# Value matmuls by seven block products, woven with the gate matmuls, and GpSimd taking over the spread sums

## The chip, the cores and the metric

The kernel runs on one core of a Trainium2 chip. The metric is the device time of one launch in microseconds (us). In one set of rounds nine executions of the kernel before lay within 0.3% of each other (546.1 to 547.48 us). One core has five engines that matter: TensorE (PE in the profile; PEld is its weight load), VectorE (DVE), ScalarE (ACT), GpSimd (POOL) and SyncE (SP), which here only issues DMAs.

## The reference

Eight batches of attention with projected keys and values are followed by a gated feed-forward layer over all 8192 tokens.

```python
k_proj = einsum('ks,bhsd->bhkd', E, k)           # 8 batches, 8 heads, 1024 -> 64 positions
v_proj = einsum('ks,bhsd->bhkd', F, v)
attn   = softmax(q @ k_proj.T / 8)
x      = (attn @ v_proj)                         # reshaped to 8192 tokens x 512
gate   = 1 / (1 + exp(-(x @ w_gate)))            # 512 -> 1536
val    = x @ w_val                               # 512 -> 1536
out    = (gate * val) @ w_out                    # 1536 -> 512
```

Nearly all of the arithmetic lies in the last three products. The kernel works on 16 blocks of 512 tokens, two for each batch.

## The kernel before

The output product already uses a Strassen-like scheme: a 2x2 block product by seven instead of eight smaller products, with sums of the operands made first ("spread sums" S1 to S4 of the hidden layer, T1 to T4 of the weights). The gate and the value still use plain matmuls.

```python
def mstep(blk, m):                     # one feature tile: 4 gate and 4 value matmuls, 512 columns
    pbs = {n: ffn.next() for n in "GV"}
    for n in "GV":
        for i in range(NI):
            mm_one(blk, m, i, n, pbs[n])
    gate(blk, m, pbs["G"], pbs["V"])   # tanh on ACT, (1 + t) * value on DVE

def s_sums(blk, n, ms):                # the sums of the hidden layer, on VectorE
    ...
    o, a, b, op, r, w = {
        1: (S1, A21, A22, ALU.add, "A21 A22", "S1"),
        2: (S2, S1, A11, ALU.subtract, "S1 A11", "S2"),
        3: (A21, A11, A21, ALU.subtract, "A11 A21", "A21"),
        4: (A12, A12, S2, ALU.subtract, "A12 S2", "A12"),
    }[n]
    dve(lambda e: e.tensor_tensor(o, a, b, op), ...)

def first_products(blk):               # the first five of the seven output products
    product(blk, a, "A11", "B11", True)
    keep_snap(0, a)
    product(blk, c, "A12", "B21", True, True)
    add_snap(0, c, 0, 0)
    for ms in ((0, 3), (3, 6)):
        s_sums(blk, 4, ms)
    product(blk, a, "S2", "T2")        # the third: reads S2
    keep_snap(1, a)
    product(blk, c, "S1", "T1", True)
    product(blk, a, "A21", "T3")       # the fifth: reads S3, which lies in A21
    ...

def gather():                          # reciprocals of the softmax sums to four partitions
    for i in range(4):
        add("SP", lambda e, i=i: e.dma_start(rrow[::32, i, :], rden[i::32, :]), ...)

def spread(rnd):                       # ... and from there to all: 16 broadcasts on GpSimd
    for j in range(4):
        n = 4 * rnd + j
        for c, parts in ((1, P), (0, 64)):
            pool(lambda e, ...: e.partition_broadcast(rb[0:parts, n, :], rrow[...], channels=parts), ...)

def mul(r, g, bk=None):                # attention outputs times the spread reciprocals
    dve(lambda e: e.tensor_tensor(xT[s][...], xu[:, n, :], rb[:, n, :], ALU.mult), ...)
```

Everything is placed by hand: `put(i, fn)` hangs a piece of attention behind the i-th feature tile. Each engine gets its instructions in program order, and semaphores are set wherever one engine needs what another made. A product of TensorE stands in a bank; an eviction is the instruction of ScalarE or VectorE that takes it out, so that the bank comes free for another product, and a snapshot is a copy taken in this way.

The softmax here doesn't subtract the row's maximum and nothing guards it: scores larger than these inputs give would overflow.

Of the kernel before, what the change touches and what calls it, by code (L numbers as in the profile page):

```python
# [118 lines left out]
def bass_linformer_attn__then__ffn_glu_sigmoid_kernel(  # L119
# [18 lines left out]
    with contextlib.ExitStack() as es:  # L138
# [5 lines left out]
        count = sbuf("count", [P, P], FP32)  # L144
        quad = sbuf("quad", [P, 1], FP32)
        row_f = sbuf("row_f", [P, 1], FP32)
        pats = sbuf("pats", [P, 4, 32], FP32)
        rows = sbuf("rows", [P, 4, 32], FP32)
        half = sbuf("half", [P, 2], FP32)
        identf = sbuf("identf", [P, P], FP32)  # L150
        ident = sbuf("ident", [P, P], BF16)
        dsel = sbuf("dsel", [P, 2, 2, 32], BF16)
        dsel8 = sbuf("dsel8", [P, 2, 4, 32], BF16)
        bsel8 = sbuf("bsel8", [P, 4, 2, 64], BF16)
        bsel8f = sbuf("bsel8f", [P, 4, 2, 64], FP32)
# [5 lines left out]
        KV = [sbuf(f"KV{i}", [P, H, S // P * DH], BF16) for i in range(2)]  # L161
        kp = sbuf("kp", [P, NR, DH], BF16)
# [5 lines left out]
        rden = sbuf("rden", [P, 512], FP32)  # L168
        rhi = sbuf("rhi", [P, 512], BF16)
        rhl = sbuf("rhl", [P, 512], BF16)  # L170
# [4 lines left out]
        rb = sbuf("rb", [P, 8, 512], FP32)  # L175
# [6 lines left out]
        sig = [sbuf(f"sig{i}", [P, 512], FP32) for i in range(3)]  # L182
# [4 lines left out]
        snap = [EF[:, 0:512], EF[:, 512:1024], sbuf("snap2", [P, 512], FP32)[:, :]]  # L187

# [28 lines left out]
        ffn, att = Ring(FB), Ring(AB)  # L217

# [119 lines left out]
        def constants():  # L338
# [61 lines left out]
            for t, k, m, w in ((dsel8, "dsel8", 8, 4), (dsel, "dsel", 4, 2)):  # L400
                for n in range(2):
                    for i in range(w):
                        dve(
                            lambda e, t=t, m=m, n=n, i=i: e.tensor_scalar(
                                t[:, n, i, :].rearrange("p (a b) -> p a b", b=m),
                                count[:, 0:m].unsqueeze(1).to_broadcast([P, 32 // m, m]),
                                half[:, n : n + 1],
                                2.0 * i,
                                op0=ALU.subtract,
                                op1=ALU.is_equal,  # L410
                            ),
                            ["count", ("half", n)],
                            [(k, n)],
                        )
# [117 lines left out]
        def half_unit(hf, ring):  # L532
# [86 lines left out]
            def bc(R):  # L619
# [17 lines left out]
                def keep(g):  # L637
                    act(
                        rb[:, 2 * R + g, :],
                        bank[bks[g]][:, :],  # L640
                        [],
                        [("rb", 2 * R + g)],
# [19 lines left out]
            def xo(R):  # L662
# [14 lines left out]
                for g in range(2):  # L677
# [3 lines left out]
                    elif R == 0:  # L681
                        scale(R, g, bank[bks[g]], rb[:, n, :], [("rb", n)], bks[g])
                if hf == 0 and R == 1:
                    for r in (2, 3):
                        for g in range(2):
# [5 lines left out]
                                    rb[:, 2 * R + g, cc],  # L691
                                    ALU.mult,
                                ),
                                [("rb", 2 * R + g)],
# [57 lines left out]
        def keep_vd(bk):  # L752
            for g in range(2):
                act(
                    vpD[64 * g : 64 * g + 64, :, :].rearrange("p h d -> p (h d)"),
                    bank[bk][64:128, :],
                    [],
                    [("vpD", h, g, R) for h in range(2) for R in range(2)],
                    b=bk,
                )  # L760

        def attention(b):
# [39 lines left out]
            def den():  # L802
                bk = att.next()
                for rnd in range(2):
                    for j in range(4):
                        n = 4 * rnd + j
                        mm(
                            bk,
                            bank[bk][32 * j : 32 * j + 32, :],
                            dsel[:, n % 2, rnd, :],  # L810
                            eT[:, n, :],
                            [("dsel", n % 2), ("eT", n)],
                            start=(rnd == 0),
                            stop=(rnd == 1),
                            tp=(0, 32 * j),
                        )
                den_bank.append(bk)

# [9 lines left out]
            def den8():  # L828
                bk = att.next()
# [51 lines left out]
            def gather():  # L881
                for i in range(4):
                    add(
                        "SP",
                        lambda e, i=i: e.dma_start(rrow[::32, i, :], rden[i::32, :]),
                        r=[("rden", c, R) for c in range(4) for R in range(2)],
                        w=[("rrow", i)] + [("eT", 2 * i + x) for x in range(2)],
                        dma=f"rrow{i}",
                    )

            def spread(rnd):
# [3 lines that stand above are left out]
# [4 lines left out]
                            r=[("rrow", 2 * rnd + c)]  # L899
                            + [("eT", 4 * rnd + 2 * c + x) for x in range(2)],  # L900
                            w=[("rb", n)],
# [21 lines left out]
            def mul(r, g, bk=None):  # L923
# [9 lines left out]
                    [("xu", n)] + ([("rb", n)] if bk is None else []),  # L933
# [13 lines left out]
            def scores():  # L947
                f, a0, a1 = two(ffn), two(att), two(att)
                order = (0, 1, 2) if b == 1 else (2, 0, 1)
# [15 lines left out]
            def outputs():  # L965
# [4 lines left out]
                if 2 < b + 1 < B:  # L970
                    held["kv"] = att.next()
                    kv(b + 1, held["kv"])
                den8() if b == 1 else den()
# [3 lines left out]
            if b == 1:  # L977
# [13 lines left out]
            return [  # L991
                scores,
                lambda: exp_one(1, held["sc"]),
                mixed,
                lambda: keep_x(1, held["x"]),
                outputs,
                lambda: (keep_x(3, held["x"]), rec(1)),
                lambda: (rec(2), keep_kd(held["kv"]) if b + 1 < B else None),
                lambda: (rec(3), gather(), keep_vd(held["kv"]) if b + 1 < B else None),
                lambda: (spread(0), spread(1)),  # L1000
                lambda: mul2(0),
                lambda: mul2(1),
                lambda: mul2(2),
                lambda: mul2(3),
            ]
# [50 lines left out]
        def gate(blk, m, pg, pv):  # L1056
# [3 lines left out]
                sg[:, :], bank[pg][:, :], [], [("sig", M % 3)], b=pg, func=AF.Tanh, scale=0.5  # L1060
# [4 lines left out]
                    sg[:, :],  # L1065
# [5 lines left out]
                [("sig", M % 3)],  # L1071
# [4 lines left out]
        def oproj(blk, tt, pb, cols=((0, DM),)):  # L1076
            o = ost[:, tt, :]
            t = 2 * (2 * (blk % 2) + tt % 2) + tt // 2
            for n, (c0, c1) in enumerate(cols):
                if n:  # L1080
                    pb = ffn.next()
# [17 lines left out]
                )  # L1099
                add(  # L1100
# [24 lines left out]
        def s_sums(blk, n, ms):  # L1125
# [11 lines left out]
            dve(  # L1137
                lambda e: e.tensor_tensor(o, a, b, op),  # L1138
                [k for x in r.split() for k in part(blk, x, up)],
                [k for k in part(blk, w, up)],  # L1140
# [32 lines left out]
        def keep_snap(n, bk):  # L1173
            act(snap[n], bank[bk][:, :], [], [("snap", n)], b=bk, scale=0.5)
# [23 lines left out]
        def first_products(blk):  # L1198
            a, c = ffn.next(), ffn.next()
# [5 lines left out]
            for ms in ((0, 3), (3, 6)):  # L1205
                s_sums(blk, 4, ms)
# [5 lines left out]
            add_snap(2, c, 1, 1)  # L1212

        def last_products(blk):
# [6 lines left out]
            ffn.next(), ffn.next()  # L1221
            for tt in (2, 3, 0, 1):
# [6 lines left out]
                )  # L1229

# [61 lines left out]
        def sums(blk, m):  # L1292
            if m >= 9 and 1 <= blk < 2 * B - 1:
                s_sums(blk, m - 8, (0, 3))
            if m <= 2 and blk >= 2:
                s_sums(blk - 1, m + 1, (3, 6))
            if blk == 2 and m <= 3:
                t_sums(m)

        for b in range(B):  # L1300
            todo = []
            for blk in (2 * b, 2 * b + 1):
                ms = [[m] for m in range(NF)]
                if blk <= 1:
                    ms = [[0, 1]] + ms[2:]
                gaps = {11: [0, 1, 2, 3]} if blk == 1 else {}
                for m in ms:
                    if len(m) == 2:
                        todo.append(
                            lambda blk=blk: first_pair(blk, None if blk else lambda: xo(1))  # L1310
                        )
                    else:
                        todo.append(lambda blk=blk, m=m[0]: (mstep(blk, m), sums(blk, m)))
                    if blk >= 2 and m[-1] == 3:
                        todo.append(lambda blk=blk: first_products(blk - 1))
                    if blk >= 2 and m[-1] == 4:
                        todo.append(lambda blk=blk: last_products(blk - 1))
                    if blk >= 1:
                        for tt in gaps.get(m[-1], ()):
                            todo.append(lambda blk=blk, tt=tt: oproj(blk - 1, tt, ffn.next()))  # L1320
            at = {}

            def put(i, fn):
                at.setdefault(i, []).append(fn)

            if b == 0:
                qt2, sc2, den2, bc2, xo2 = half_unit(1, att)
                put(4, lambda: (qt2(0, ("DVE", "ACT")), qt2(1, ("DVE", "ACT"))))
                put(5, lambda: (sc2(0), sc2(1)))
                put(5, second_loads)  # L1330
                put(7, lambda: (den2(), xo2(0), xo2(1)))
                put(9, lambda: (bc2(0), bc2(1)))
                spots = (12, 14, 15, 16, 17, 18, 19, 19, 20, 21, 23)
            elif b == 1:

                def kv2():
                    bk = att.next()
                    kv(2, bk)
                    keep_kd(bk)
                    keep_vd(bk)  # L1340
# [58 lines left out]
```

## Time and profile before

| | before |
|---|---|
| time, median of 4 | 547.59 us (547.53 to 548.18) |
| TensorE busy | 530.7 us, 97% of the span |
| VectorE, ScalarE, GpSimd busy | 56%, 43%, 21% |
| period of a steady batch | 64.6 us |
| granted TensorE clock | 1.000 |

A timeline line reads: start, duration, engine, source line, operation, output<-inputs, shape, count, and in brackets the idle time ahead of it with what ended that idle time.

### The profile page before, as it was taken

How to read it: one execution, taken by the hardware profiler on the slowest of the kernel's cores; microseconds unless marked ns; L12 is line 12 of the kernel's file. 1: busy time of each engine (PE TensorE's matmuls, PEld its weight loads, DVE VectorE, ACT ScalarE, POOL GpSimd, SP SyncE). 2: the span in 40 equal slices, each digit the busy share in tenths (PEclk: the TensorE clock that was granted, in tenths of full speed). 3: DMA queues.
4: the chain of work that ended last, by engine and by line, in shares of the span. 5: the costliest groups of instructions: out<-in, count | busy, mean ns of one | idle time of the engine just before them, and what ended most of it. 6: DMA issues, size and time to landing. Idle time of an engine off the chain costs nothing.

```text
span 545.4 us, 8923 instructions
## 1 busy us (share of the span) xinstructions
PE 530.7 (97%) x3504; PEld 298.7 (55%) x3561; DVE 305.5 (56%) x499; ACT 232.1 (43%) x414; POOL 113.5 (21%) x148
## 2 busy tenths in 40 slices
PE   5999999999999999999999999999999999999998
PEld 4544445646565474644647465564656547474654
DVE  4645386346863559437583466734785375834432
ACT  2654823465335633365333753346533562323330
POOL 9310200103800055000830019000350007100000
PEclk9999999999999999999999999999999999999999
DMA  9999998983795117960286502953020202001022
GB/s 159 200 195 201 163 209 176 153 178 49 148 201 127 31 21 150 152 156 11 79 137 131 121 12 78 185 144 59 13 78 1 78 0 81 2 7 72 1 77 78
DMA packets 76570, 56.09 MB, mean 103 GB/s; under 512 B 34704, under 2 KB 68240, under 8 KB 76528
## 3 DMA queue, kind: packets, MB, share of 16 engines
q0 software_dynamic: 33984, 29.89, 35.4%
q1 hardware_dynamic: 42544, 25.63, 18.6%
q8 instruction: 28, 0.46, 0.4%
q14 instruction: 14, 0.11, 0.1%
HBM read 60.29 MB, written 16.78 MB: 141 GB/s over the span
## 4 chain that ended last, share of the span: by engine, by line
PE 93%; DMA 2%; DVE 1%; ACT 1%; issue 1%; POOL 1%; POOLq 0%
PE pF L227 88%; PE pA L227 5%; DMA KV<-in_v_dram 2%; DVE hT L1063 0%; DVE rden L822 0%; POOL KV L245 0%; POOL Qb L245 0%; ACT xu L231 0%; ACT vpD L231 0%; ACT sig L231 0%; ACT eT L231 0%; ACT kpd L231 0%; DVE rden L602 0%; DVE hS L1138 0%; DVE xT L651 0%
## 5 line engine op out<-in xcount | busy, mean ns | idle before, releaser
L1063 DVE SCALAR_TENSOR_TENSOR hT<-sig,pF 128x512 bf16<-128x512 f32 x192 | 130.6, 681 | 118.9 <-PE pF L227 75.1
L227 PE MATMUL pF<-xT,wV 128*128 128x512 bf16 x752 | 195.6, 379 | 1.2 <-DVE hT L1063 0.3
L227 PE MATMUL pF<-xT,wG 128*128 128x512 bf16 x729 | 191.2, 379 | 3.1 <-issue 1.3
L231 ACT ACTIVATE sig<-pF 128x512 f32<-128x512 f32 x192 | 116.1, 605 | 171.2 <-PE pF L227 146.6
L896 POOL PARTITION_BROADCAST rb<-eT x96 | 77.1, 864 | 279.6 <-DMA eT<-rden 274.5
L227 PEld LDWEIGHTS pF<-xT,wV 128*128 128x128 bf16 x768 | 75.0, 98 | 90.9 <-DVE hT L1063 1.0
L227 PEld LDWEIGHTS pF<-xT,wG 128*128 128x128 bf16 x768 | 72.6, 98 | 88.6 <-issue 9.0
L227 PE MATMUL pF<-wO,hT 128*128 128x256 bf16 (+3 forms) x610 | 80.8, 287 | 0.1
L227 PEld LDWEIGHTS pF<-wO,hT 128*128 128x128 bf16 x612 | 59.2, 98 | 19.7 <-issue 0.8
L1183 DVE SCALAR_TENSOR_TENSOR ost<-pF,EF 128x512 f32<-128x512 f32 x28 | 19.4, 692 | 51.4 <-PE pF L227 48.8
L227 PE MATMUL pF<-wT,hT 128*128 128x256 bf16 x336 | 41.2, 273 | 0.0
L927 DVE TENSOR_TENSOR xT<-xu,rb 128x512 bf16<-128x512 f32 x48 | 40.3, 878 | 0.0
L227 PE MATMUL pF<-wT,hS 128*128 128x256 bf16 x336 | 39.0, 273 | 0.3 <-ACT EF L231 0.3
L231 ACT ACTIVATE EF<-pF 128x512 f32<-128x512 f32 x28 | 16.7, 597 | 47.0 <-PE pF L227 46.9
L227 PEld LDWEIGHTS pF<-wT,hT 128*128 128x128 bf16 x336 | 32.9, 98 | 6.8
L227 PEld LDWEIGHTS pF<-wT,hS 128*128 128x128 bf16 x336 | 32.8, 98 | 4.3 <-ACT EF L231 0.6
L822 DVE RECIPROCAL rden<-pA 128x128 f32<-128x128 f32 x26 | 24.6, 950 | 9.5 <-PE pA L227 9.5
L1183 DVE SCALAR_TENSOR_TENSOR ost<-pF,snap 128x512 f32<-128x512 f32 x14 | 9.7, 692 | 35.6 <-PE pF L227 25.0
L231 ACT ACTIVATE xu<-pA 128x512 f32<-128x512 f32 x46 | 25.2, 617 | 1.1 <-PE pA L227 1.1
L231 ACT ACTIVATE snap<-pF 128x512 f32<-128x512 f32 x14 | 8.4, 597 | 28.3 <-PE pF L227 28.3
L231 ACT ACTIVATE eT<-pA 128x512 bf16<-128x512 f32 x35 | 19.3, 622 | 1.0 <-PE pA L227 1.0
L231 ACT ACTIVATE eT<-pF 128x512 bf16<-128x512 f32 x29 | 15.8, 594 | 8.3 <-PE pF L227 8.2
(93 smaller groups left out, 268.5 us busy)
## 6 DMA issues: line engine op xcount, KB each, us to landing
out_dram<-ost SPq DMA_DIRECT2D x63, 256.0 KB, 2.4
Qb<-in_q_dram POOLq DMA_DIRECT2D x7, 1024.0 KB, 17.8
KV<-in_k_dram POOLq DMA_DIRECT2D x7, 1024.0 KB, 9.8
KV<-in_v_dram POOLq DMA_DIRECT2D x7, 1024.0 KB, 14.0
wO<-in_moe_w_out_dram POOLq DMA_DIRECT2D x1, 1536.0 KB, 11.9
wG<-in_moe_w_gate_dram POOLq DMA_DIRECT2D x5, 256.0 KB, 18.2
wV<-in_moe_w_val_dram POOLq DMA_DIRECT2D x5, 256.0 KB, 18.8
KV<-in_k_dram POOLq DMA_DIRECT2D x2, 512.0 KB, 8.8
```

The source lines that it names most:

```text
L227: return add("PE", lambda e: e.matmul(o, lhsT, rhs, **kw), r=r, x=[("bank", b)])
L231: return add("ACT", lambda e: e.activation(o, i, func, scale=scale), r=r, w=w, x=x)
L822: lambda e: e.reciprocal(rden[:, cc], bank[bk][:, cc]),
L896: lambda e, n=n, i=2 * rnd + c, j=j, parts=parts: e.partition_broadcast(rb[0:parts, n, :], rrow[32 * j : 32 * j + 1, i, :], channels=parts),
L927: lambda e: e.tensor_tensor(xT[s][:, r, :, 256 * g : 256 * g + 256], xu[:, n, :].rearrange("p (f c) -> p f c", f=2), y.rearrange("p (f c) ...
L1063: lambda e: e.scalar_tensor_tensor(hT[blk % 2][:, m, :], sg[:, :], 1.0, bank[pv][:, :], ALU.add, ALU.mult,),
L1183: lambda e: e.scalar_tensor_tensor(o, bank[bk][:, :].rearrange("p (j c) -> p j c", j=2), 0.5, snap[n].rearrange("p (j c) -> p j c", j=2), ...
```

## The change

It wants fewer matmul columns: the value product of 14 of the 16 blocks also goes by seven products, in pieces woven between gate matmuls. VectorE gets the additions that this needs (products added to snapshots, and sums of the blocks of the input x, the x sums, `xS` in the profile), so the hidden-layer sums S1 to S3 go to GpSimd. Attention visits are placed anew in six units per batch; memory is found by letting the broadcast results share the tiles of K and V.

```diff
-        KV = [sbuf(f"KV{i}", [P, H, S // P * DH], BF16) for i in range(2)]
+        KVs = sbuf("KVs", [P, 2, H, S // P * DH], BF16)
+        KV = [KVs[:, i, :, :] for i in range(2)]
+        rb = (KVs[:, :, :, :] ... .bitcast(FP32) ...)      # broadcast results share K and V
...
-                for i in range(4):                          # gather: 4 DMAs
+                for m in range(8):                          # now 8 of half the size
...
-        def s_sums(blk, n, ms):
+        def s_sums(blk, n, ms, eng="DVE"):
...
+        def v_pieces(K):                                    # one unit: 7 products of 4 matmuls
+            def p1():
+                v_product(blk, q, a, "A11", "B11", start=True)
+                v_snap(0, a)                                # ACT copies the bank
+            def p26():
+                v_product(blk, q, c, "A12", "B21", start=True, stop=True)
+                v_add(0, c)                                 # DVE adds to the copy
+                v_product(blk, q, a, "S2", "T2")
+                ...
+        for b in range(1, B):
+            for u in range(6):                              # six units per batch
+                todo += [last_piece, p1, g_step 1, p26, g_step 2, p57, g_step 3, p4, next g_step 0]
...
+            def pool_sums(blk, ms):
+                for n in (1, 2, 3):
+                    s_sums(blk, n, ms, "POOL")
+            if b > 1:
+                on(0, 2, lambda: pool_sums(o0, (4, 6)))
+            on(2, 4, lambda: pool_sums(o1, (0, 4)))
+            on(3, 2, lambda: pool_sums(o1, (4, 6)))
+            if b + 1 < B:
+                on(5, 4, lambda: pool_sums(o1 + 1, (0, 4)))
...
+                on(3, 0, n["outputs"])                      # issues gather, then 16 broadcasts
...
+                on(5, 0, lambda: first_products(o1, hook))  # hook: six multiplies
```

`on(u, j, fn)` places work in unit u behind its j-th piece. The outputs, with the broadcasts, sit at (3, 0), and the sums of the last two feature tiles at (3, 2).

## The prediction

> **What bounds the kernel now.** I read the page's busy shares and its chain that ended last, then the TensorE timeline of one steady batch.
>
> ```profile
> span 545.4 us, 8923 instructions
> PE 530.7 (97%) x3504; PEld 298.7 (55%) x3561; DVE 305.5 (56%) x499; ACT 232.1 (43%) x414; POOL 113.5 (21%) x148
> ...
> PE 93%; DMA 2%; DVE 1%; ACT 1%; issue 1%; POOL 1%; POOLq 0%
> ```
>
> TensorE is 97% of the span and 93% of the chain, so time comes off only with matmul columns. Busy time doesn't give the cost of a matmul, since matmuls overlap; the cadence, start to start, does:
>
> ```profile
> 351.96 2.78 PE L227 MATMUL pF<-wO,hT 128*128 128x256 bf16 x24
> 354.58 2.78 PE L227 MATMUL pF<-wT,hS 128*128 128x256 bf16 x24
> ...
> 362.85 1.03 PE L227 MATMUL pF<-xT,wG 128*128 128x512 bf16 x4
> 363.72 1.03 PE L227 MATMUL pF<-xT,wV 128*128 128x512 bf16 x4
> ```
>
> A group of four 512-column matmuls takes 0.864 us (362.85 to the next group at 364.58), one 256-column matmul 2.62/24 = 0.109 us, so weight loads at 256 columns are hidden. A steady batch takes 64.6 us (broadcasts begin at 325.31 and again at 389.92): 48 groups are 41.4, the 14 output products of 12 x 0.109 are 18.35, the three attention visits 1.1, 0.9 and 3.05. That sums to the batch: there are next to no waits.
>
> The second path to know is that of the softmax sums, which is hidden now:
>
> ```profile
> 386.57 0.95 DVE L822 RECIPROCAL rden<-pA 128x128 f32<-128x128 f32 x1
> 387.55 2.34 SPq L885 DMA_DIRECT2D eT<-rden  x4
> 389.92 0.79 POOL L896 PARTITION_BROADCAST rb<-eT  x1 [48.16 <-DMA eT<-rden]
> 390.88 6.38 POOL L896 PARTITION_BROADCAST rb<-eT  x8 [0.16 <-POOL rb L896]
> 397.42 6.21 POOL L896 PARTITION_BROADCAST rb<-eT  x7 [0.16 <-POOL rb L896]
> 398.36 1.98 DVE L927 TENSOR_TENSOR xT<-xu,rb 128x512 bf16<-128x512 f32 x2
> 401.88 2.15 DVE L927 TENSOR_TENSOR xT<-xu,rb 128x512 bf16<-128x512 f32 x2
> 405.33 1.29 DVE L927 TENSOR_TENSOR xT<-xu,rb 128x512 bf16<-128x512 f32 x2
> ```
>
> Gather issues cost SyncE 0.58 us each; the broadcast waits for the second (issued by 1.17) and starts at 2.37, so landing takes 1.2 us. The 16 broadcasts take 389.92 to 403.63, 13.7 us. Two multiplies take 1.29 us alone but 1.98 and 2.15 beside broadcasts.
>
> [...] In the timeline GpSimd's instructions indeed run in program order.
>
> **The change, part by part, per batch.**
>
> Removed: 24 value groups, 24 x 0.864 = 20.7 us. Added: 7 products x 6 units x 4 matmuls of 256 columns, 168 x 0.109 = 18.35 us. TensorE work falls by 2.4 us a batch, in 7 batches: 16.6 us, 3.0%. This is the intended gain; TensorE's batch becomes 62.2 us.
>
> VectorE: the 24 gate operations stay 24 hidden-layer ones of the same size; 18 additions of a product to a snapshot come (0.6 each when queued, like the eviction of 0.69 whose successor starts 0.60 later), +10.8; 8 input sums of about 0.4, +3.2; two reciprocals less, -1.8; twelve of the sixteen half-size output sums (0.47 queued) leave for GpSimd, -5.6, and the rest merge. From about 40 to 47 of 62 us. ScalarE: 18 more snapshots at 0.49 queued, 28 to 37 us. Neither becomes the bound on average. Within a unit the tightest reuse is the third snapshot, needed again after one gate group of 0.86 us: start 0.2 after the product, 0.6 long, just enough. I allow 0.3 us a batch.
>
> GpSimd: the output sums S1, S2, S3 now run there, in one piece of 4 and one of 2 feature tiles per block. [...] With 13.7 of broadcasts and 2.7 of load issue it is busy some 37 of 62 us: free on average, but FIFO, and here I expect the loss.
>
> **The wait that I think replaces the gain.** In a batch, the attention outputs are visited at the start of unit 3. Call that 0. The sum matmuls end at 1.1, plus 0.24 to VectorE; two reciprocals (0.87 + 0.95) end at 3.2. The gather is now 8 DMAs, and the first broadcast needs the second and sixth: 6 x 0.58 + 1.2 = 4.7, so 7.9. Broadcasts until 21.6. Only then, since they stand behind the broadcasts in program order, come the sums of the last two feature tiles of the finished block: S1 until about 22.9, S2 about 24.2, S3 25.5.
> TensorE meanwhile: attention 3.05, rest of unit 3 6.1, unit 4 6.5, one product 0.44: the output products of that block start at 16.1. The first two take 2.62, and the third reads S2, whose fifth tile is needed at 19.1. It comes at 24.2: TensorE stands 5.1 us, in each of the six batches 1 to 6. Against 2.4 saved, a batch gets 2.7 us longer.
>
> Batch 6 loses more: its next attention has no K/V projection (1.9 us), which in the five others lies inside this latency path, so it loses 4.6. Batch 7 has no attention and keeps -2.1.
>
> On top comes exclusion. After S2, GpSimd runs S3 and then at once the large sums[...] of the next block, while VectorE has the in-place sum, six multiplies with two SBUF inputs, and behind four of them the eviction that the last output product needs. Unhindered that eviction ends some 4 us after S2, needed at about 6[...]. I put 2 us a batch, from 0 to 6, also for VectorE's backlog at the turn of the batch.
>
> Once, before unit 0 of batch 1, VectorE gets 4 value-weight and 4 output-weight sums (0.87 queued), output-block sums and input sums during 11 us of plain output projection that also needs 8 multiplies (0.6) and 4 evictions (0.6). I count its queue to end about 8 us after TensorE is through with the projection; the first eviction of a product stands behind it, while the three products before take 4: +4 us.
>
> Sharing memory between the broadcast results and K/V costs nothing by itself: loads go out at the start of a batch after the multiplies, and land by the page's issue table within 18 us; the projection reads them some 25 us later.
>
> Sum: batches 1 to 5: 5 x (2.7 + 2 + 0.3) = 25; batch 6: 6.9; batch 7: -2.1; turn +4. Together some +34. I shade this to +28, because exclusion may be milder and GpSimd's sums quicker than the estimate: **575 us**.
>
> **The rivals.** First, the plain one: TensorE stays the bound and the 16.6 us arrive, 531 us. For it speaks that every engine keeps slack on average; against it that the broadcasts, 13.7 us in a row, with 8 us ahead of them, are measured durations and the S2 instructions stand behind them. Even sums that cost only 0.5 us each leave a 3.5 us wait against a gain of 2.4.
> Second, GpSimd sums quick and exclusion harmless: 6 batches of +1 to +1.5, batch 6 a further +2, turn +2 to +4, batch 7 -2: 555 to 560, at the edge of "same".
> Third, VectorE or ScalarE becomes the bound through its order, each unit stretching: 47 of 62 us speaks against a pure throughput bound, but in unit 5 of a batch VectorE has about 15 us of work in 15.7 us. [...]
> Fourth, a load that comes late because K/V memory is free later: 25 us against 18 speaks against it; it would add to the same waits at the outputs visit.
>
> **Range and chances.** The floor of the mechanism is about 556, the full-exclusion case about 602; I take 556 to 602. Slower by over 2% is above 558.5: 0.83. Faster by over 2% needs the FIFO argument to be wrong altogether: 0.04. The rest 0.13.
>
> **What would show it.** Right: third output products in the last unit of batches 1 to 6 that begin, run four matmuls and stop for about 5 us on POOL; gathers of 8 issues, 4.6 us; GpSimd sums directly after the broadcasts; TensorE's busy share down to some 90%; matmul cadence still 0.109; multiplies and in-place sums stretched beside GpSimd's sums. Wrong: TensorE above 95% busy, a batch period below 63 us, S2 sums finishing before the third product; or GpSimd sums that take well under 1 us; or waits found mainly on VectorE evictions within units, which would mean I mis-sized that side.

Cut from the record, at the marks, are rules and figures that no trace had shown, among them the length of GpSimd's sums. In the changed kernel a sum took 1.14 to 1.48 us for 512 elements (1.92 for one right behind the broadcasts), 2.11 to 2.64 for 1024, and GpSimd was busy for 37.5 us of the batch shown below. The times of S1 to S3 and the 37 us rest on the cut lengths, and the 2 us a batch for exclusion on an estimate that no trace sized; all of these are the author's estimates. Exclusion means that VectorE and GpSimd hold each other up; the trace of before had two multiplies at 1.98 and 2.15 us beside broadcasts instead of 1.29, and run 2 below shows more. The sum is 25 + 6.9 - 2.1 + 4, some +34, shaded to +28, so 575 us. "The page's issue table" is that of the profile page of before: 17.8 us to landing for a load of Q.

## More of the kernel before

The kernel's text asks for the library with the broadcast once, early in the program.

The profile page draws each engine as a row of 40 equal slices of the span, with the busy share of a slice in tenths; the clock row is the TensorE clock that was granted, also in tenths. These are two of the rows of the kernel before:

```profile
PE   5999999999999999999999999999999999999998
PEclk9999999999999999999999999999999999999999
```

After the first slice TensorE is never idle for long, and its clock never drops.

## The result, and the profile after

The changed kernel took **685.26 us** (median of 4; 684.15 to 686.27) against 547.59 of the kernel before in the same rounds (547.53 to 548.18). The ratio is 1.2511, with a 95% interval of 1.2487 to 1.2534. All ratios in this document divide the mean time of one kernel's fast runs by that of the other's in the same rounds, so they differ a little from the ratio of the medians quoted. The prediction had the direction, but 685 lies far outside 556 to 602.

The page of the changed kernel, in the lines that answer to those of before (spans, busy shares, the two rows, the chain):

```profile
span 682.4 us, 10389 instructions
PE 549.8 (81%) x4113; PEld 356.1 (52%) x4113; DVE 400.3 (59%) x577; ACT 301.2 (44%) x540; POOL 257.7 (38%) x226
...
PE   5999976792979929899288991889928998379998
PEclk9999987896889969899698996989969999599999
...
PE 10%; DVE 2%; issue 1%; POOL 0%; ACT 0%; POOLq 0%; DVEq 0%
```

TensorE fell from 97% to 81%, with a notch in its row once per batch (a 1, 2 or 3 tenths), and at each notch the clock row shows 5 or 6 tenths. The chain accounts for only 13% of the span: it broke off early when followed back, so it is of no use here, and the totals of waits take its place (engine and line, waited for: us in total, times, longest):

```profile
PE pA L263 <- POOL hS L1226: 81.0, 6, 14.3
...
POOL hS L1226 <- issue: 42.6, 6, 7.6
...
PE pF L263 <- DVE vsnap L1429: 31.0, 13, 4.7
```

Six waits of TensorE for GpSimd's sums, one for each of batches 1 to 6, cost 81 us. The second line is the odd one: GpSimd itself sat idle six times for up to 7.6 us, for nothing that the profile shows.

The TensorE timeline of the batch whose broadcasts start at 399.35:

```profile
410.05 0.60 PE L263 MATMUL pA<-wT,hS 128*128 128x256 bf16 x4
424.32 4.45 PE L263 MATMUL pA<-wT,hS 128*128 128x256 bf16 x20 [13.66 <-POOL hS L1226]
428.56 1.79 PE L263 MATMUL pA<-wT,hT 128*128 128x256 bf16 x12
430.19 0.60 PE L263 MATMUL pF<-xT,wV 128*128 128x256 bf16 x4
...
437.17 0.61 PE L263 MATMUL pF<-xS,wV 128*128 128x256 bf16 x4 [1.16 <-DVE vsnap L1429]
...
445.78 1.44 PE L263 MATMUL pF<-xT,wG 128*128 128x512 bf16 x4 [3.65 <-DVE vsnap L1429]
```

The first two output products have run by 410.05, the third does four matmuls and then stops for 13.66 us. It goes on slowly: the 20 matmuls after the stop take 4.24 us (424.32 to 428.56), where the cadence of before, 0.109 us, would give 2.18. The granted clock was 1.00 from 410.66 to 415.50, 0.50 from 415.60 to 429.10, and 1.00 again from 429.30 to 446.20.

GpSimd's timeline of the same batch says what the 13.66 us are made of:

```profile
399.35 0.80 POOL L916 PARTITION_BROADCAST KVs<-eT  x1 [11.84 <-PE pF L263]
400.35 7.35 POOL L916 PARTITION_BROADCAST KVs<-eT  x8 [0.19 <-POOL KVs L916]
407.89 6.41 POOL L916 PARTITION_BROADCAST KVs<-eT  x7 [0.19 <-POOL KVs L916]
421.89 1.14 POOL L1226 TENSOR_TENSOR hS<-hT 128x512 bf16<-128x512 bf16 x1 [7.60 <-issue]
423.11 1.15 POOL L1226 TENSOR_TENSOR hS<-hS,hT 128x512 bf16<-128x512 bf16 x1
```

The last broadcast ends at 414.30; S1 starts at 421.89 and S2 ends at 424.26, and TensorE resumes at once. Between broadcasts and sums lie 7.60 us of nothing. VectorE was idle in all of this time; its next instruction is the sum that needs S2:

```profile
424.30 0.96 DVE L1226 TENSOR_TENSOR hT<-hT,hS 128x1536 bf16<-128x1536 bf16 x1 [13.25 <-POOL hS L1226]
```

**The batch adds up.** Without waits it would be 64.6 - 2.4 = 62.2 us. The stop adds 13.66; slow matmuls after it 2.38 (4.24 instead of 2.18, then 1.63 instead of 1.31); the two later waits 1.16 and 3.65; slow matmuls after the last of them 1.70 (the weave from 445.78 to 450.07, 4.29 us instead of 2.6, at a granted clock of 0.50 from 446.30 to 449.60). The sum is 84.8, and the batch took 85.3 (399.35 to 484.65); 0.5 us are not assigned.

Two stops came once, in batch 1: 3.52 us for an eviction behind VectorE's queue at the turn (the +4 of the prediction), and 6.01 us for the transposed keys of the next batch, whose DMA, issued at 106.30, came behind the three loads of K, V and Q issued from 104.48; in run 8, where the loads wait for these keys, the stop is gone. The prediction hadn't seen the second.

### The profile page after: what moved, and what is told of

Read it like the earlier page. It is cut to its first block, busy times and chain, and to the rows that moved or that the text cites. A ratio compares the mean times of both kernels' runs of the same rounds, so it can differ in the third digit from the quotient of the medians.

```text
span 682.4 us, 10389 instructions
## 1 busy us (share of the span) xinstructions
PE 549.8 (81%) x4113; PEld 356.1 (52%) x4113; DVE 400.3 (59%) x577; ACT 301.2 (44%) x540; POOL 257.7 (38%) x226
## 5 line engine op out<-in xcount | busy, mean ns | idle before, releaser
L1429 DVE TENSOR_TENSOR vsnap<-pF,vsnap 128x512 f32<-128x512 f32 x126 | 86.6, 688 | 83.3 <-PE pF L263 59.5
L263 PE MATMUL pA<-wT,hS 128*128 128x256 bf16 x336 | 52.2, 322 | 84.5 <-POOL hS L1226 81.0
L263 PEld LDWEIGHTS pF<-xT,wG 128*128 128x128 bf16 x768 | 75.1, 100 | 81.3 <-DVE vsnap L1429 22.9
L916 POOL PARTITION_BROADCAST KVs<-eT x96 | 82.1, 881 | 81.4 <-PE pF L263 61.9
L267 ACT ACTIVATE vsnap<-pF 128x512 f32<-128x512 f32 x126 | 75.3, 597 | 70.6 <-PE pF L263 63.8
L1410 DVE SCALAR_TENSOR_TENSOR hT<-sig,vsnap 128x512 bf16<-128x512 f32 x126 | 95.2, 756 | 5.8
L263 PE MATMUL pF<-xT,wV 128*128 128x256 bf16 (+1 forms) x432 | 78.2, 303 | 0.3 <-DVE hT L1149 0.3
L263 PE MATMUL pF<-xS,wV 128*128 128x256 bf16 x336 | 51.7, 278 | 10.0 <-DVE vsnap L1429 9.8
L263 PE MATMUL pA<-wO,hT 128*128 128x256 bf16 x504 | 59.6, 273 | 0.0
L263 PE MATMUL pF<-xS,vT 128*128 128x256 bf16 x336 | 53.2, 283 | 0.0
L948 DVE TENSOR_TENSOR xT<-xu,KVs 128x512 bf16<-128x512 f32 x48 | 52.0, 1132 | 0.0
## 6 DMA issues: line engine op xcount, KB each, us to landing
Qb<-in_q_dram POOLq DMA_DIRECT2D x7, 1024.0 KB, 17.8
KVs<-in_v_dram POOLq DMA_DIRECT2D x7, 1024.0 KB, 13.7
```

Of the source, the lines that this page charges most:

```text
L263: return add("PE", lambda e: e.matmul(o, lhsT, rhs, **kw), r=r, x=[("bank", b)])
L267: return add("ACT", lambda e: e.activation(o, i, func, scale=scale), r=r, w=w, x=x)
L916: lambda e, n=n, i=2 * rnd + c, j=j, parts=parts: e.partition_broadcast(rb[0:parts, n, :], rrow[32 * j : 32 * j + 1, i, :], channels=parts),
L948: lambda e: e.tensor_tensor(xT[s][:, r, :, 256 * g : 256 * g + 256], xu[:, n, :].rearrange("p (f c) -> p f c", f=2), y.rearrange("p (f c) ...
L1410: lambda e: e.scalar_tensor_tensor(o, sg[:, :, cc], 1.0, x.rearrange("p (j c) -> p j c", j=2), ALU.add, ALU.mult,),
L1429: lambda e: e.tensor_tensor(o, bank[bk][:, :], o, ALU.add),
```

## The experiments

My theory after the trace: (T) GpSimd in order puts S2 behind 16 broadcasts, as predicted, but two terms were missing. One is a pause of about 7 us whenever GpSimd goes from a broadcast to a two-input sum; the other is the TensorE clock, which drops in such a stop. The rivals: (R1) the pause is the tail of the broadcasts, or a wait for VectorE; (R2) the cost is the mutual exclusion of VectorE and GpSimd, whatever the order on GpSimd; (R3) the seven-product values cost the time themselves, through evictions, and GpSimd is a side show.

**1. All spread sums on VectorE.** This takes away the order on GpSimd and the exclusion by sums.

```diff
-                    s_sums(blk, n, ms, "POOL")
+                    s_sums(blk, n, ms, "DVE")
```

> The changed kernel with all output-block sums (S1, S2, S3) on VectorE at the same places instead of GpSimd. Theory (the loss is GpSimd's queue: sums behind 13.7 us of broadcasts, a gap of 7 us after them, and exclusion against VectorE): the stop of 13.8 us at the third output product and VectorE's stretched input sums at the end of a batch go; the mean clock returns to above 0.98; a batch takes 62 to 66 us instead of 85; in all 545 to 565 us. Rival (the 7-product values weave itself is too tight in banks and snapshots, so VectorE with 53 of 62 us becomes the bound): a batch stays above 72 us and the run above 600 us.

Measured, 3 rounds: 568.33 us (565.12 to 569.09), ratio to the kernel before 1.0379 (1.0346 to 1.0413), clock 0.991. That is slightly above the 545 to 565 us expected. So GpSimd's sums carry about 117 of the 138 us lost, and R3 can carry at most the other 21. The third product isn't interrupted any more. Of the 21, the turn (3.52 us) and the late keys (6.41) are two single waits; the steady batch is 65.5 us (332.57 to 398.08) instead of 62.2, with short waits for VectorE late in the batch.

**2. Only the two-tile sums behind the broadcasts on VectorE.**

```diff
-            on(3, 2, lambda: pool_sums(o1, (4, 6)))
+            on(3, 2, lambda: [s_sums(o1, n, (4, 6)) for n in (1, 2, 3)])
```

> The changed kernel with only the three small sums behind the broadcasts (last two feature tiles of the even block) moved to VectorE; the other nine groups stay on GpSimd. Theory that the position behind the broadcasts is what costs: the 13.8 us stop goes, and with it most of the cold clock; what is left of the loss is exclusion between GpSimd's large sums and VectorE at the end of a batch (5 us) : 570 to 600 us. Rival that GpSimd's sums cost by exclusion wherever they stand: still above 630 us.

Measured, 3 rounds: 610.11 us (608.02 to 612.45), ratio 1.1169 (1.1139 to 1.1198), clock 0.949. The time missed the 570 to 600 us expected, and lies below the rival's 630: the exclusion that stays was taken too small. The stop in the third product is gone, which is worth 75 us, more than half the loss. What is left shows the exclusion on its own, at the end of the batch. From the timelines of VectorE (first fence) and GpSimd (second):

```profile
384.18 2.29 DVE L1410 SCALAR_TENSOR_TENSOR hT<-sig,vsnap 128x512 bf16<-128x512 f32 x1
386.39 2.33 DVE L1372 TENSOR_TENSOR xS<-xT 128x512 bf16<-128x512 bf16 x1
```

```profile
383.81 2.11 POOL L1226 TENSOR_TENSOR hS<-hT 128x1024 bf16<-128x1024 bf16 x1 [7.33 <-DVE vsnap L1429]
386.00 2.45 POOL L1226 TENSOR_TENSOR hS<-hS,hT 128x1024 bf16<-128x1024 bf16 x1
```

For each sum on GpSimd one VectorE instruction gets in, so an x sum that takes 0.42 us alone lasts as long as a GpSimd sum, 2.2 to 2.3 us. TensorE then waits 8.10 us for the eviction behind them. R2 is therefore real, but it is the second cost: it isn't what stops the third product.

**3 and 4. The pause by itself, in the kernel before.** Two scratch sums that nobody reads are put behind the broadcasts of the kernel before (3), or between their two halves, with a memset behind the second half (4).

```diff
-                lambda: (spread(0), spread(1)),
+                lambda: (spread(0), spread(1), scratch_sum(0), scratch_sum(1)),                    # 3
+                lambda: (spread(0), scratch_sum(0), scratch_sum(1), spread(1), scratch_zero()),    # 4
```

The expectations of 4 to 6 call the pause a reload. What GpSimd does in a pause was not shown.

> The kernel before with two idle sums of 128x512 bf16 in scratch memory on GpSimd, right behind the 16 broadcasts of each batch. Theory (GpSimd pays once when it goes from broadcasts to an ordinary tensor operation[...]): a gap of 7 us before the first sum, none (0.1 us) before the second, in each of six batches, though VectorE has a different load here. Rival (the gap is exclusion by VectorE operations, or belongs to that place of the changed kernel): a gap below 2 us, or one that varies with VectorE's work. Time within 1% of before in both.

> The kernel before with two idle sums between the first and last eight broadcasts, and a memset behind the last. Theory of a reload at each change of kind: about 7 us before the first sum, 0.1 before the second, and again some us before the ninth broadcast (6 to 8 if the way back costs the same, under 1 if only the way to ordinary operations costs); 7 us before the memset if any ordinary operation needs the reload. Rival (the broadcast's own tail of about 7 us): 7 us before the sum and before the memset, nothing before the ninth broadcast. Time 550 to 575 us, since multiplies come up to 15 us later.

Measured, one look each: 547.75 us (3) and 612.65 us (4). The time of run 4 missed its 550 to 575 us, as its multiplies came later than expected; its pauses are as the theory has them. GpSimd in run 3, then in run 4:

```profile
217.53 2.76 POOL L247 TENSOR_TENSOR scr_o<-scr 128x512 bf16<-128x512 bf16 x2 [7.39 <-issue]
```

```profile
222.00 2.37 POOL L247 TENSOR_TENSOR scr_o<-scr 128x512 bf16<-128x512 bf16 x2 [6.80 <-issue]
230.29 0.80 POOL L910 PARTITION_BROADCAST rb<-eT  x1 [5.91 <-issue]
231.26 6.38 POOL L910 PARTITION_BROADCAST rb<-eT  x7 [0.17 <-POOL rb L910]
237.70 0.52 POOL L253 MEMSET scr_o<- 128x512 bf16 x1
```

The pause stands without any change to the matmuls, ahead of the first of two sums and not of the second (6.80 to 7.81 us, twelve times in the two runs), and again on the way back to a broadcast (5.75 to 6.01 us, six times). A memset behind a broadcast starts at once, and these sums wait for no data. That rules out R1: the pause on the way back follows sums, so it is no tail of a broadcast, and in the changed kernel VectorE was idle through the pause shown, so it held nothing up. It is a cost of changing between the two operations, in both directions.

The traces also hold a mark of the change, though the views leave it out. Read directly, the packed traces list the instructions of GpSimd's sequencer, and at the start of each of these pauses stand two MODIFY_POOL_CONFIG instructions with the source line of the coming sum or broadcast: in run 4 at 215.11 before the sum and at 224.57 before the broadcast, and none before the memset or between the two sums. The kernel before has one such pair in all, for the one load of the library in its text, and so none where loads of K, V and Q are issued right behind broadcasts; run 3 has 12 pairs, run 4 has 13, the changed kernel 14, and the kernels without sums on GpSimd (runs 1, 8 and 9) one. So in these runs a pair comes at every change, though the kernel's text asks for the library once. Each pause follows such a pair, and only the first operation pays it: 5.75 to 6.01 us on the way to a broadcast, 6.60 to 7.81 in all runs on the way from a broadcast to a sum.

In run 3 it is hidden, and in run 4 it lies in the path of the multiplies, so it adds 65 us to a kernel whose arithmetic is unchanged.

**5. Half of the broadcasts.** If the pause is fixed, half of the broadcasts take away only their own 7 us.

```diff
-                    for c, parts in ((1, P), (0, 64)):
+                    for c, parts in ((1, P),):
...
-                            r=[("rrow", 2 * rnd + c, x) for x in range(2)]
+                            r=[("rrow", 2 * rnd + y, x) for x in range(2) for y in range(2)]
```

The second cut makes each broadcast left wait for the gather of both; the last DMA that the first broadcast waits for stays the sixth.

> The changed kernel with only 8 of the 16 broadcasts of a batch (the results are wrong on purpose; the timing of everything else is unchanged). Theory (stop at the third output product = broadcasts' length + a reload of 7 us + sums, minus what TensorE does meanwhile): broadcasts end 6.6 to 7 us earlier, the gap of 7 to 7.6 us behind them stays, the stop falls from 13.8 to about 7 us, the run from 685 to 635 to 650 us. Rival without a reload (a fixed end time set by something else): the gap shrinks or grows to fill, stop still above 11 us or gone.

Measured, one look: 646.86 us, and the result still passed the comparison. The pauses are 6.66 to 7.21 us, as with 16 broadcasts. TensorE's six stops for these sums come to 35.0 us instead of 81.0. One of them:

```profile
319.53 4.24 PE L263 MATMUL pA<-wT,hS 128*128 128x256 bf16 x20 [5.16 <-POOL hS L1226]
```

46 us in six stops are 7.7 each, about what eight broadcasts take (14.95 us for 16), so the pause remained. And behind a stop of 5.16 us, 20 matmuls take 4.07 us (the next group starts at 323.60), nearly the 4.24 after the long one: the clock loss hardly grows with the stop.

**6. No broadcasts at all** (the result is wrong, relative error 5.48; the multiplies wait for the gather and read what lies in the tile).

```diff
-                    for c, parts in ((1, P), (0, 64)):
+                    for c, parts in ():
...
```

> The changed kernel with no broadcasts (wrong results on purpose): all sums stay on GpSimd[...]. Theory (reload comes from the alternation with broadcasts): no gap of 7 us anywhere on GpSimd, no stop at the third output product; exclusion between GpSimd's sums and VectorE's two-input operations at the end of a batch stays, with single VectorE operations of 1.2 to 2.5 us; 590 to 625 us. Rival (exclusion is minor): below 570 us, near the run with all sums on VectorE.

Measured, one look: 606.14 us. No pause is left on GpSimd, and the third product runs through. What stays is the exclusion and a clock of 0.955. From here it becomes plain how little idle time can cost the clock; this is the last of the seven output products of a batch in that run:

```profile
309.55 2.71 PE L263 MATMUL pA<-wO,hT 128*128 128x256 bf16 x12 [2.07 <-DVE ost L1279]
```

Behind a stop of 2.07 us, 12 matmuls took 2.51 us (the next group starts at 312.06) instead of 1.31. The trace's clock record has TensorE at half its clock for 3.41 us from 309.62, just after it resumed.

**7. Keeping TensorE busy in the stop.** If the dropped clock costs about 4 us per batch, filling the stop with matmuls that nobody reads should win it back.

```diff
+        def warm(n):
+            for _ in range(n):
+                mm(FF[0], bank[FF[0]][:, 0:256], ident[:, :], wO[:, 0, 0:256], ["ident", "wO"])
...
             s_sums(blk, 4, (0, 6))
+            warm(fill)                                      # 100 in batches 1 to 6
```

> The changed kernel with 100 idle 256-column matmuls (10.9 us) into a free bank just before the third output product of each of the six batches, to fill the stop of 13.8 us. Theory (the clock of TensorE drops during a long stop and the matmuls behind it run at half speed for some 4 us): the matmuls after the stop keep 0.109 us each, the mean clock rises from 0.91 to 0.95 or more, and the run gets 2 to 2.5 us shorter in each of six batches: 670 to 675 us. Rival (the slow matmuls after the stop are due to late operands): no change, or slower by what the fill doesn't hide.

Measured, 3 rounds: 696.84 us (693.3 to 701.71), ratio to the kernel before 1.2737 (1.2687 to 1.2787). This was a miss: the filling fitted, the clock rose from 0.912 to 0.956, and the kernel is slower than the changed one by about 12 us. TensorE, VectorE and GpSimd in the same batch, each in its own timeline:

```profile
332.97 11.08 PE L263 MATMUL pF<-wO,ident 128*128 128x256 bf16 x100
...
346.85 2.36 PE L263 MATMUL pA<-wT,hS 128*128 128x256 bf16 x20 [2.36 <-POOL hS L1226]
...
357.58 2.74 PE L263 MATMUL pA<-wO,hT 128*128 128x256 bf16 x12 [4.45 <-DVE ost L1278]
```

```profile
347.70 9.22 DVE L948 TENSOR_TENSOR xT<-xu,KVs 128x512 bf16<-128x512 f32 x4
```

```profile
349.16 2.16 POOL L1226 TENSOR_TENSOR hS<-hT 128x1024 bf16<-128x1024 bf16 x1 [0.37 <-PE pA L263]
```

The 20 matmuls are fast again (2.36 us instead of 4.45). Start to start they take 2.19 us behind a stop of 2.36, and in another batch of this run 2.20 behind a stop of 2.46, while run 6 had slow ones behind 2.07: the length of a stop alone doesn't decide it. But the next block's sums on GpSimd may start as soon as these matmuls have read S2 and S1, since they overwrite them. Now they start at 349.16, 1.46 us into VectorE's four multiplies, which therefore take 9.22 us. In the same batch of the changed kernel the slow matmuls held those sums back until 343.22, when the multiplies that began at 339.88 were just done, after 3.44 us. The saved 2 us turned into a new stop of 4.45 us, behind which the clock is down again; such a stop came in three of the six batches. So the clock loss is real, but in these batches of the changed kernel the slow matmuls happened to shield VectorE from GpSimd; the two costs can't be added as independent ones.

**8. A new order without GpSimd sums.** All sums go to VectorE in whole pieces. From batch 2 on, the attention outputs come one unit earlier and the first block's output products one later, and multiplies are spread over both blocks. The next loads wait until the multiplies are done and the keys are transposed, and the eight gather DMAs go in the order in which the broadcasts need them. The sums at the turn move between the products.

```diff
-                for m in range(8):
+                for m in (1, 5, 0, 4, 3, 7, 2, 6):
...
-            on(3, 2, lambda: pool_sums(o1, (4, 6)))
+            on(3, 6, lambda: s_sums(o1, 1, (0, 6)))
+            on(4, 3, lambda: s_sums(o1, 2, (0, 6)))
+            on(4, 5, lambda: s_sums(o1, 3, (0, 6)))
...
+                on(uo, 0, n["outputs"])                     # uo = 2 for b >= 2
...
+                    on(3, 0, lambda: first_products(o0, mul2))
+                    on(3, 4, lambda: mul2(2))
+                    on(4, 1, lambda: mul2(3))
```

> Seven-product values kept, made to fit: all output-block sums on VectorE, one whole piece each and spread over the first two and the fourth unit; the attention outputs visited one unit earlier, so broadcasts end under the output products of the odd block and the multiplies lie there too; loads at the end of the batch before; gather DMAs in the order in which broadcasts need them; value-weight sums of the start behind the first eviction. Theory: TensorE is the bound again, a batch takes 62.2 to 63 us, the mean clock is 0.99 or more, 531 to 540 us. Rival (the value weave has waits of its own that add up): a batch above 64.6 us, 547 us or more.

Measured, 5 rounds: 553.43 us (552.52 to 555.53), ratio 1.0116 (1.0094 to 1.0138), clock 1.000. Both the time and the batch are in the rival's range and not in the theory's. The long stops are gone, among them the turn and the late keys, but a batch still takes 66.1 us. The rest is in short waits where VectorE has multiplies and sums together:

```profile
325.80 0.61 PE L263 MATMUL pF<-xS,wV 128*128 128x256 bf16 x4 [0.58 <-DVE vsnap L1429]
...
331.00 0.61 PE L263 MATMUL pF<-xS,wV 128*128 128x256 bf16 x4 [0.96 <-DVE vsnap L1429]
```

**9. The same, with VectorE's work moved to where it was idle.** Two of the four multiply pairs go into the next output products, the x sums go later and in halves, and the next loads are issued a little later, behind them.

```diff
-                    on(3, 4, lambda: mul2(2))
-                    on(4, 1, lambda: mul2(3))
-                    on(5, 0, lambda: first_products(o1))
-                    on(5, 1, lambda: [xs_sums(o1 + 2, n) for n in (1, 2, 3, 4)])
+                    on(5, 0, lambda: first_products(o1, lambda i: mul2(2 + i)))
+                    on(5, 4, lambda: [xs_sums(o1 + 2, n) for n in (1, 2)])
+                    on(5, 6, lambda: [xs_sums(o1 + 2, n) for n in (3, 4)])
```

> The run before this one (the seven-product values with all spread sums on VectorE and the attention outputs one unit earlier) took 553.4 us, with a batch of 66.1 us, of which matmuls account for about 62.4 us; TensorE's short stops of 0.4 to 1.0 us behind VectorE's copies stood in the units right after the first output products, where VectorE did two multiplies per head pair beside its sums. This run moves the last two pairs of multiplies into the next output products, where VectorE was idle for 2.9 and 1.1 us, and moves the x sums of the second block one unit on. Theory that VectorE's order within the batch, not its total, held the 1-percent loss: a batch of 62.6 to 63.8 us, 535 to 545 us in all, clock 0.99 or above, so faster than before. Rival, that the seven-product values cost TensorE as much in waits for VectorE's added evictions (72 percent busy) as they save, wherever the rest stands: a batch of 65 us or more and 548 to 555 us.

Measured, 5 rounds: **535.66 us** (535.35 to 537.52) against 546.44 of the kernel before (546.1 to 547.48, 9 runs), ratio 0.9808 (0.9792 to 0.9825), clock 1.000. This is faster than both kernels; as the interval reaches across 0.98, it is unclear whether it is faster by 2%. Its page and two starts of broadcasts, one batch apart:

```profile
PE 522.5 (98%) x4113; PEld 345.9 (65%) x4113; DVE 395.7 (74%) x616; ACT 300.6 (56%) x540; POOL 128.9 (24%) x148
```

```profile
297.71 0.81 POOL L916 PARTITION_BROADCAST KVs<-eT  x1 [26.12 <-PE pF L263]
...
360.48 0.81 POOL L916 PARTITION_BROADCAST KVs<-eT  x1 [26.10 <-PE pF L263]
```

A batch takes 62.8 us, within 0.6 of the 62.2 that matmul columns ask for, and no TensorE wait above 0.9 us is left after the first 60 us. With the values by seven products and VectorE at 74%, R3 falls as well: 10.8 of the intended 16.6 us arrived once the work on the other engines stood elsewhere. Runs 8 and 9 change several places at once, so they don't tell what each is worth.

## Why the prediction was wrong, and where it was right

Right, by its own steps:

- **The gain.** 2.4 us per batch and 62.2 us of matmuls: the cadence of 0.109 us stayed, and run 9 comes to 62.8 us per batch.
- **The mechanism.** It named the third output product of the last unit, four matmuls in, waiting on POOL, in each of batches 1 to 6. Its clock starts at the outputs visit (391.40 in the batch shown): first broadcast predicted at 7.9, measured 7.95; TensorE's stop predicted at 19.1, measured 19.25; the three sums predicted at 3.9 us in all, measured 4.37 (421.89 to 426.26); over the run a sum took 1.14 to 1.48 us for 512 elements (1.92 for S3 behind the broadcasts, where VectorE works too) and 2.11 to 2.64 for 1024. Run 2 confirms it by taking these sums out of GpSimd's line.
- **The turn.** +4 us, measured 3.52. The waits of TensorE show none that comes from sharing memory with K and V.

Wrong:

- **The step that failed** is "Only then, since they stand behind the broadcasts in program order, come the sums ...: S1 until about 22.9, S2 about 24.2", which gave "TensorE stands 5.1 us". S2 ended at 32.86. Of the 8.6 us more, 7.6 are the pause between broadcast and sum, which runs 3 and 4 show on their own, and about 1.3 the broadcasts (14.95 us instead of 13.7). The prediction had no term for the change from broadcasts to sums; its own sign of being right, "GpSimd sums directly after the broadcasts", did not come. The term was mis-sized by a factor of 2.7, in six batches: 81 us measured, 31 predicted.
- **The clock was left out.** The working took the cadence of 0.109 for granted on both sides of a stop. The stops cost about 4 us per batch in slow matmuls (2.38 + 1.70 above). As a check on the whole kernel: the same 4113 matmuls are busy 549.8 us here and 522.5 us in run 9, 27 us apart. In the stop shown the granted clock went from 1.00 to 0.50, and the 20 matmuls behind it took 4.24 us instead of 2.18.
- **Exclusion was mis-sized.** "I put 2 us a batch"; the later waits for evictions were 1.16 + 3.65 us in the batch shown, and 31 us in all. The place was another, too: the prediction put the wait at the eviction that the last output product needs, and in the changed kernel TensorE never waited there (it did in runs 6 and 7, for 2.07 and 4.45 us). It waited for additions to snapshots: 1.16 us behind multiplies, and 3.65 us behind the x sums at the end of the batch, beside GpSimd's sums for the next batch's first output block. These x sums weren't in its list.
- **The late keys** (6.01 us once) weren't foreseen: the prediction looked for loads that land late for the projection, and not for another DMA queued behind them.
- **The shading.** Its own sum was +34; it was shaded to +28 because sums and exclusion might be milder. Nothing in the profile supported that, and every term that it had not foreseen lay on the slow side.

Added up from the views named, the waits are 81.0 + 31.0 + 3.5 + 6.0, the clock 27, the gain -16.6: together +132 of the measured +138. The remaining 6 us are not assigned, and run 7 shows that these terms depend on each other. The pause on the way back to a broadcast costs nothing in the changed kernel: its MODIFY_POOL_CONFIG pair stands at 387.70, right behind GpSimd's last sum (387.51), and GpSimd had 11.84 us without work until the first broadcast at 399.35, which starts 4.67 us after the gather's first DMA, as landing alone would have it.

## What to carry to other kernels

An engine that is free on average isn't free for a different kind of work: ask what stands ahead in its queue, and measure what it costs to change from one operation to another (here 6.60 to 7.81 us from a broadcast to a sum), best with two idle instructions put into the kernel as it is; here MODIFY_POOL_CONFIG in the trace marked the change. When an estimate has a wait on TensorE in it, add the slow matmuls after it (here about 4 us a batch), from a trace that has such a stop. The scheme that saves matmuls paid here only when its added evictions and sums fell into idle stretches of VectorE, so move such work piece by piece with the timeline at hand: here the same arithmetic took 685, 568, 553 and 536 us.
